# Attention and a two-layer network on one core: the network's input kept on chip as float16 parts, chunks of 256 tokens, weight scales by groups of four blocks

## The chip, the cores and the metric

The kernel runs on one core of one Trainium2 chip. A core has a matrix engine (PE), a vector engine (DVE), a scalar engine (ACT), a general engine (POOL), and a queue (SP) that issues DMAs. The metric is the time on the device in microseconds. The kernel before took 1076.19 us (median of three runs, 1075.35 to 1078.62).

## The reference

Attention over 8 batches, 8 heads, 576 positions and 64 features, with a causal mask and a decay bias from running sums of `s`; then a network of 512 to 2048 to 512 features over all 4608 tokens. All of it in float32; the two weight matrices arrive in 8-byte floats.

```python
scores = scale * np.matmul(q, k.transpose(0, 1, 3, 2))
s_pos = np.maximum(s, 0.0)
cum = np.cumsum(s_pos, axis=-1)
bias = -(cum[:, :, :, None] - cum[:, :, None, :])
scores = np.where(causal, -1000000000.0, scores + np.minimum(bias, 0.0))
attn = softmax(scores)                       # rows, with 1e-9 added to the sum
x = (attn @ v).transpose(0, 2, 1, 3).reshape(4608, 512)
h = x @ w_in
g = np.where(h > 0.0, h, np.exp(np.minimum(h, 0.0)) - 1.0)
out = g @ w_out
```

## The kernel before

All work is written down as operations (`op`), each with a priority, one or more ways (an engine and an assumed cost), and the tiles that it reads and writes. `Plan.issue` then puts them in one order: at each step it takes the operation that could start earliest by its assumed costs, and among equals the one with the lowest priority number. Every engine executes its own operations in that order, and so does SP with its DMAs. A tile has a tag and a number of buffers (`bufs`); its first writer can be issued only when a buffer of the tag, or of one of its `others`, is free.

Attention goes by pairs of heads (`j` is 0 to 3). Batches 0 to 2 are cut: their first 320 positions ("low", classes `Low`, `prepare_low`, `scoring_low`, `weighing_low`) are worked in full float32 at the start; then come batches 3 to 7 whole (`prepare`, `scoring`, `weighing`, one unit for the first 64 rows of both heads and one for each head), and last the other 256 positions of batches 0 to 2. Scores are made in PSUM banks (`score_bank`, tag `a`, two buffers; while the network isn't at work also the banks of `h` and `o0` to `o2`), the maximum is taken on DVE (L972), the exponent on ACT (L977), the weights are split into two float16 parts (L1022 to L1030), turned by DMA and multiplied with the values (L1131) into the one bank `av`. From there the result is copied to SBUF (L1143, L1145, or `psum_copy` for low units) and stored to `x_dram`, features by tokens.

The network goes by 12 chunks of 384 tokens in the order in which attention makes them. Chunk 0 is native: float32 products, each two records in the trace (L1301 for the hidden layer, L1346 for the output). It can begin as soon as a weight block is there. The other chunks take three float16 products instead of one float32 product (high by high, high by low, low by high; L1317 and L1354). For that `load_x` brings a chunk back from `x_dram`, and it is scaled by a power of two and split into `xh` and `xl` (L402 to L404 and L1270). For each of 16 blocks of 128 hidden features, `elu` and what follows take the bank of `h` through ACT and DVE: exponent (L1281), clamp (L1288 or L1292), maximum (L1326), high part (L1330 or L1332), low part (L1335). The 12 products of a block go into `h` (two banks), the 9 of its output into three banks that collect over all 16 blocks.

Weights come in 32 units of 512 KB (`load_unit`): a DMA into one of two raw tiles (tag `io`), one operation on ACT (L638) and two on DVE (L641, L644) that make float32 of 8-byte floats, and the largest magnitude (`peak`, L575 on DVE or L578 on ACT). When all 32 are there, `weight_scales` makes one scale for each matrix (two small products through PE in `scales_of`, L609 and L612), and `split_unit` makes the float16 parts (L402 or L403, then L659).

## Time and profile before

| | |
|---|---|
| median of three runs | 1076.19 us |
| profiled execution, its span | 1076.1 us |
| mean granted clock of TensorE | 0.990 |
| PE, PEld, DVE, ACT, POOL busy | 96%, 55%, 80%, 59%, 41% |
| HBM read, written | 79.66 MB, 19.32 MB |

The span is the time from the first to the last instruction of one profiled execution; nothing of note lies around it, as it equals the runs' median. Times in the profile are in microseconds, and those marked ns, or the middle number of a triple like 322/326/543, in nanoseconds. L1317 is line 1317 of the kernel. PEld is the loading of weights into the matrix engine. In a stretch's line each engine has its busy time and, in brackets, the number of its instructions; PEclk is the clock that TensorE was granted, as a share of full speed. In a group's line the name left of the arrow is the tile that is written, then the shape, the count, busy time and mean length, and behind it the idle time ahead of the group with what ended it. Ends of matmuls are modelled, so their cadence is read from their starts.

### The profile page before, as it was taken

Reading aid. Unit: us, or ns where it says so; the run is one execution under the profiler, and the core shown is the slowest. Engines: PE = TensorE matmul, PEld = TensorE weight load, DVE = VectorE, ACT = ScalarE, POOL = GpSimd, SP = SyncE. Lnnn points to the kernel's source line nnn. Section 1 sums busy time; section 2 is a strip of 40 time slices with the busy share of each in tenths; the row PEclk is TensorE's granted clock in tenths of the full one; section 3 lists DMA queues with packets and bytes.
Section 4 is the critical chain, followed back from the end, with each engine's and each line's share of the span. In section 5 each row is a group of like instructions: output and inputs, shape, how many; then the busy total and the mean of one; then the engine's idle time right before and its main releaser. Section 6 shows DMA issues by size and latency. Waiting matters only on the chain.

```text
span 1076.1 us, 19708 instructions
## 1 busy us (share of the span) xinstructions
PE 1028.8 (96%) x6014; PEld 597.0 (55%) x6014; DVE 859.3 (80%) x2216; ACT 640.2 (59%) x1511; POOL 443.2 (41%) x687
## 2 busy tenths in 40 slices
PE   8899999899799999999999999999999999999998
PEld 7555555345455555555555555555555655555554
DVE  7787988998788988898898888988898998442433
ACT  5787675547566666655656666665556566444443
POOL 6542443525365645454535545444444544000000
PEclk9999999899899999999999999999999999999999
DMA  6776889526667675675579675867765567210000
GB/s 192 216 223 203 213 213 203 139 65 142 172 149 193 149 171 136 169 179 147 120 168 191 144 162 137 195 159 167 170 168 143 143 156 148 52 60 1 30 1 30
DMA packets 295097, 156.52 MB, mean 145 GB/s; under 512 B 214200, under 2 KB 269776, under 8 KB 294992
## 3 DMA queue, kind: packets, MB, share of 16 engines
q1 hardware_dynamic: 294992, 155.27, 58.5%
q8 instruction: 48, 0.79, 0.3%
q14 instruction: 57, 0.47, 0.2%
HBM read 79.66 MB, written 19.32 MB: 92 GB/s over the span
## 4 chain that ended last, share of the span: by engine, by line
PE 70%; DVE 16%; issue 5%; DMA 4%; ACT 2%; POOL 2%; SPq 1%; DVEq 0%; POOLq 0%; ACTq 0%
PE o L1354 24%; PE h L1317 23%; PE sc L969 8%; PE av L1131 5%; DVE p L1030 4%; PE o L1346 3%; PE h L1301 2%; DVE xl L1270 2%; DVE h L1326 2%; DVE wp L659 1%; DVE gg L1335 1%; DVE p L972 1%; PE trl L791 1%; DMA T<-p 1%; DMA stq<-in_qT_dram 1%
## 5 line engine op out<-in xcount | busy, mean ns | idle before, releaser
L1317 PE MATMUL h<-xh,wp 128*128 128x384 f16 x1408 | 394.1, 329 | 19.4 <-DVE gg L1335 14.0
L1354 PE MATMUL o<-wp,gg 128*128 128x512 f16 x1584 | 390.6, 382 | 0.0
L1317 PEld LDWEIGHTS <-wp 128*128 128x128 f16 x2112 | 198.0, 98 | 177.0 <-issue 35.8
L1317 PE MATMUL h<-xl,wp 128*128 128x384 f16 x704 | 230.8, 328 | 3.9 <-DVE xl L1270 3.9
L1354 PEld LDWEIGHTS <-gg 128*128 128x128 f16 x1584 | 147.2, 99 | 154.0 <-issue 6.8
L1281 ACT ACTIVATE g<-h,cs 128x384 f32<-128x384 f32 x176 | 101.8, 578 | 156.3 <-PE h L1317 145.4
L977 ACT ACTIVATE p<-p,mn 128x192 f32<-128x192 f32 (+1 forms) x232 | 144.2, 622 | 56.6 <-DVE mn L972 49.2
L1326 DVE SCALAR_TENSOR_TENSOR h<-g,cs,h 128x384 f32<-128x384 f32 x176 | 108.5, 617 | 86.8 <-ACT g L1288 85.7
L1030 DVE SCALAR_TENSOR_TENSOR p<-p,sm,p 128x512 f16<-128x512 f32 (+3 forms) x237 | 168.9, 736 | 3.2 <-POOL p L1022 1.1
L1330 ACT ACTIVATE gg<-h 128x384 f16<-128x384 f32 x155 | 75.4, 487 | 93.2 <-DVE h L1326 91.6
L969 PE MATMUL sc<-kh,qs 128*128 128x192 f32 (+2 forms) x272 | 120.0, 444 | 7.7 <-DVE mn L972 7.3
L972 DVE CUSTOM_DVE_ANT_0 p<-sc,maskw 128x192 f32<-128x192 f32 (+1 forms) x232 | 109.6, 480 | 18.8 <-PE sc L969 14.3
L1022 POOL TENSOR_SCALAR p<-p,sm 128x512 f16<-128x512 f32 (+3 forms) x120 | 79.5, 670 | 95.5 <-DVE sm L983 34.0
L1335 DVE SCALAR_TENSOR_TENSOR gg<-h,gg 128x384 f16<-128x384 f32 x176 | 96.9, 550 | 22.0 <-ACT gg L1330 19.3
L969 PE MATMUL sc<-k,q 128*128 128x192 f32 (+2 forms) x272 | 84.4, 313 | 0.5 <-DMA q<-qs 0.5
L411 POOL TENSOR_TENSOR k<-stk,kh 64x576 fp32r<-64x576 f32 x49 | 73.1, 1492 | 24.4 <-ACT kh L392 19.9
L969 PEld LDWEIGHTS sc<-kh,qs 128*128 128x128 f32 x272 | 52.4, 192 | 35.6 <-DVE mn L972 14.5
L1288 ACT ACTIVATE g<-g 128x384 f32<-128x384 f32 x134 | 69.9, 522 | 3.7
L1026 ACT ACTIVATE p<-p,sm 128x512 f16<-128x512 f32 (+3 forms) x100 | 57.4, 594 | 18.5 <-DVE sm L983 8.2
L411 POOL TENSOR_TENSOR qs<-stq,qs 64x512 fp32r<-64x512 f32 (+1 forms) x46 | 52.4, 1139 | 34.0 <-ACT qs L392 23.5
L390 POOL TENSOR_SCALAR qs<-stq 128x256 fp32r<-128x256 f32 (+1 forms) x43 | 24.3, 566 | 88.8 <-PE sc L969 57.5
L1131 PE MATMUL av<-T,v 128*64 128x256 f16 (+5 forms) x896 | 60.2, 286 | 0.0
(179 smaller groups left out, 1414.1 us busy)
## 6 DMA issues: line engine op xcount, KB each, us to landing
stk<-in_kT_dram SPq DMA_DIRECT2D x64, 288.0 KB
va<-in_vb_dram SPq DMA_DIRECT2D x32, 320.0 KB
stq<-in_qT_dram SPq DMA_DIRECT2D x40, 256.0 KB
w_i<-in_w_in_dram SPq DMA_DIRECT2D x16, 512.0 KB
w_o<-in_w_out_dram SPq DMA_DIRECT2D x16, 512.0 KB
out_dram<-ost SPq DMA_DIRECT2D x32, 256.0 KB
x_dram<-x_None SPq DMA_DIRECT2D x20, 288.0 KB
q<-qs SPq DMA_DIRECT2D x40, 128.0 KB
```

Of the source, the lines that this page charges most:

```text
L411: ("Pool", pool_2(n), lambda: pool.tensor_tensor(dst(), src(), hi(), ALU.subtract)),
L969: pe_.matmul(view(sc.v[:, :cw]), l, r, start=n == 0, stop=n == len(pairs) - 1)
L972: op(prio, [("DVE", 84 + dve_p(cw), lambda i=i, sc=sc: dve.tensor_tensor_reduce(pt.v[:, i * cw : (i + 1) * cw], sc.v[:, :cw], mv(i * cw, c ...
L977: op(prio, [("ACT", 480 + w / 1.2, lambda: act.activation(pt.v[:, :w], pt.v[:, :w], AF.Exp, bias=mn.v[:, n - 1 : n], scale=-1.0, accum_out ...
L1022: ("Pool", 160 + 1.04 * n, lambda part=part: pool.tensor_scalar(part(t16, 0), own(part), sm.v[:, r], 1.0, ALU.mult, ALU.mult)),
L1030: ("DVE-SB", dve_2(n), lambda part=part: dve.scalar_tensor_tensor(part(t16, 1), own(part), sm.v[:, r], part(t16, 0), ALU.mult, ALU.subtract)),
L1131: pe_.matmul(av.v[w.h * HB : (w.h + 1) * HB, dst], w.values.v[:, w.h, kb, v], part(w, kb, m), start=kb == 0 and m == 0 and v == 0, stop=kb ...
L1281: op(side, [("ACT", act_c(TC) + (0 if native else 90), lambda: act.activation(g.v[:, :TC], hp.v[:, :TC], AF.Exp, scale=1.0 if native else ...
L1317: pe_.matmul(hp.v[:, :TC], weight_part(f, 0, part)[1]()[:, c * P : (c + 1) * P], xx.v[:, c, :TC], start=(c == 0 and m == 0), stop=(c == NC ...
L1326: op(side, [("DVE", dve_p(TC), lambda: dve.scalar_tensor_tensor(hp.v[:, :TC], g.v[:, :TC], by(2 if sign[0] else 1), hp.v[:, :TC], ALU.mult ...
L1335: op(side, [("DVE", dve_p(TC), lambda: dve.scalar_tensor_tensor(gg.v[:, 1, :TC], hp.v[:, :TC], 2.0**-DOWN, gg.v[:, 0, :TC], ALU.mult, ALU. ...
L1354: pe_.matmul(acc[i].v, gg.v[:, g, tb], weight_part(f, 1, part)[1](), start=(f == 0 and m == 0), stop=(f == NF - 1 and m == 2),)
```

## The change

- **x stays on chip.** `produce` writes the result of attention straight from the bank `av` (for the first 64 rows of a whole batch from SBUF) as a high and a low float16 part into tiles `xs` of 512 tokens, scaled by the power of two of its own group of values. There are two such tiles, and two more in the place of weight tiles once these are done with. `x_dram`, `load_x` and the operations on `xc` go. A run of tokens is cut where a tile ends, and at the ends of chunks that hold tokens of two scales; in such a chunk `input_scale` brings both to one scale in place. Low units load the values of a whole batch at its first pair, to have their scale, and their transposes are ordered behind that scale.
- **Chunks of 256 tokens**: 18 in place of 12, chunk 0 native as before, from a float32 tile `x_first`. Two blocks of hidden features share one bank of `h` and go through ACT and DVE together, 512 columns at a time. Hidden and output steps of one chunk run on into the next in one order. The output has two banks.
- **Weight scales by groups of four blocks.** Each group has its own scale and is split as soon as its four blocks are there; the low part may also be made on POOL. The output's high part is scaled by a factor that brings all groups to one scale (`common_scale`, which needs all four). The float32 weights lie in four tiles of two blocks each, which the second eight blocks use again, and there are four raw tiles in place of two.
- **PSUM banks**: three for scores in place of two, and none borrowed from the network.

The diff, cut to its core (of the native chunk, outputs and stores only names change with the size):

```diff
-N_ST, N_A, N_AV, N_H, N_IO, N_G, N_X, N_T, N_K, N_V = 2, 2, 1, 2, 2, 1, 1, 2, 2, 2
+N_ST, N_A, N_AV, N_H, N_O, N_IO, N_G, N_GG, N_X, N_T, N_K, N_V = 2, 3, 1, 2, 2, 2, 1, 3, 2, 2, 2, 2
+TC = 256
+NATIVE = True
+TX = 512
...
+N_RAW, N_LOW = 4, 5
+OPEN_H, OPEN_O = 0, 0
...
-W0, WD = 45, 3
-F_EARLY = 6
+W_PRIO = 45, 57, 69, 81
...
+    vs = plan.buf(sb, [P, N_LOW, n_low, D], F32, "vs", tag="va", bufs=2)
...
-    w_all = [plan.buf(sb, [P, W_GROUP, 2, 512], F32, f"wa_{g}") for g in range(NG)]
+    w_values = [plan.buf(sb, [P, 2, 2, 512], F32, f"wv_{n}", tag=f"wa_{n % 4}") for n in range(NF // 2)]
     w_parts = [plan.buf(sb, [P, W_GROUP, 2, 2, 512], F16, f"wp_{g}") for g in range(NG)]
+    w_raw = plan.buf(sb, [P, N_RAW, 512, 2], U32, "w_raw", tag=f"wp_{NG - 1}")
...
+    def weight_scales(g):
+        at = A_W + g * 2 * (W_GROUP + 1)
+        col = slice(2 * g, 2 * g + 2)
+        scales_of(-600, [(at, W_GROUP + 1), (at + W_GROUP + 1, W_GROUP + 1)], 2 * g)
         op(-600, [("DVE-SB", 100.0, lambda: power(
-            scales.v.bitcast(U32)[:, 3:4], scales.v.bitcast(U32)[:, 1:2], 2 * 127))],
-           [(scales, 0)], [(scales, 3)])
+            wc.v.bitcast(U32)[:, col], scales.v.bitcast(U32)[:, col], 2 * 127))],
+           [(scales, 2 * g)], [(wc, ("inverse", g))])
+    def common_scale():
+        def steps():
+            a, b = (scales.v[:, m : 2 * NG : 2] for m in range(2))
+            ab, least, back, first, r = (wc.v[:, m : n] for m, n in ((8, 12), (12, 13), (13, 14), (14, 15), (16, 20)))
+            dve.tensor_tensor(ab, a, b, ALU.mult)
+            dve.tensor_reduce(least, ab, mybir.AxisListType.X, ALU.min)
+            power(wc.v.bitcast(U32)[:, 13:14], wc.v.bitcast(U32)[:, 12:13], 2 * 127)
+            dve.tensor_scalar(first, scales.v[:, 0:1], back, 2.0**DOWN, ALU.mult, ALU.mult)
+            power(wc.v.bitcast(U32)[:, 16:20], wc.v.bitcast(U32)[:, 8:12], 2 * 127)
+            dve.tensor_scalar(r, r, least, 2.0**-DOWN, ALU.mult, ALU.mult)
+        op(-600, [("DVE-SB", 500.0, steps)], [(scales, 2 * g) for g in range(NG)], [(wc, "common")])
...
+        def in_place():
+            pool.tensor_scalar(value(), value(), scales.v[:, col], 1.0, ALU.mult, ALU.mult)
+            pool.tensor_tensor(low_v(), value(), high_v(), ALU.subtract)
+        op(prio, [
+            ("DVE-SB", dve_2(512), lambda: dve.scalar_tensor_tensor(
+                low_v(), value(), scales.v[:, col], high_v(), ALU.mult, ALU.subtract)),
+            ("Pool", pool_1(512) + pool_2(512), in_place),
+        ], [(scales, at), high], [place, low])
...
+            if f % W_GROUP == W_GROUP - 1:
+                weight_scales(f // W_GROUP)
+                for m in range(f - W_GROUP + 1, f + 1):
+                    split_unit(m, 0)
+                    split_unit(m, 1)
+        common_scale()
...
+    xs = [plan.buf(sb, [P, 2, NCB, TX], F16, f"x_{k}", tag="x", bufs=N_X,
+                   others=[(f"wa_{m}", 1, lambda n: n > 1) for m in range(2)], always=True)
+          for k in range(-(-at // TX))]
+    x_parts = [[] for _ in xs]
...
+    x_first = plan.buf(sb, [P, NCB, TC], F32, "x_first")
...
+    def spans(t0, n):
+        cuts = {t0, t0 + n}
+        for t in range(t0 // TC * TC, t0 + n, TC):
+            if t > t0 and (t % TX == 0 or len(domains(t // TC)) > 1 or len(domains(t // TC - 1)) > 1):
+                cuts.add(t)
+        cuts = sorted(cuts)
+        return list(zip(cuts, cuts[1:]))
+    def produce(prio, j, t0, n, src, reads, by, on_psum=True):
+        fixed = isinstance(by, float)
+        scale = (lambda: by) if fixed else by
+        for lo, up in spans(t0, n):
+            k, m, o = lo // TX, up - lo, lo % TX
+            x, key = xs[k], (j, lo)
+            if NATIVE and lo < TC:
+                psum_copy(prio, m, lambda lo=lo, up=up: x_first.v[:, j, lo:up],
+                          lambda lo=lo, up=up: src()[:, lo - t0 : up - t0], reads[:1], [(x_first, (j, lo))])
+                continue
+            x_parts[k].append((lo, up, j, key))
+            def dst(part, x=x, o=o, m=m):
+                return x.v[:, part, j, o : o + m]
+            def of(lo=lo, up=up):
+                return src()[:, lo - t0 : up - t0]
+            more = 0 if fixed else 90
+            if on_psum:
+                op(prio, [
+                    ("ACT", act_c(m) + more, lambda dst=dst, of=of: act.activation(
+                        dst(0), of(), AF.Copy, scale=scale())),
+                    ("DVE", dve_p(m), lambda dst=dst, of=of: dve.tensor_scalar(
+                        dst(0), of(), scale(), None, ALU.mult)),
+                ], reads, [(x, (0, *key))])
+            else:
+                scaled(prio, m, lambda dst=dst: dst(0), of, scale, reads, [(x, (0, *key))])
+            op(prio, [("DVE" if on_psum else "DVE-SB", dve_p(m), lambda dst=dst, of=of: dve.scalar_tensor_tensor(
+                dst(1), of(), scale(), dst(0), ALU.mult, ALU.subtract))],
+               reads + [(x, (0, *key))], [(x, (1, *key))])
...
+        if j == 0:
+            first = A_LOW + b * (NP + 1)
+            for n in range(NP):
+                r = (b * NP + n) % N_LOW
+                load(prio, lambda r=r: vs.v[:, r], lambda n=n: vb[b, n, :, :n_low], [], [(vs, r)], P * n_low * D * 4)
+                peak(prio, n_low * D, lambda r=r: vs.v[:, r], [(vs, r)], first + n, mybir.AxisListType.XY)
+            low_scale[b] = group_scale(prio, first, S_LOW + 2 * b)
...
+            produce(prio, u.j, start[u.b, False], LOW, lambda: av.v[:, :LOW], [av, (scales, col)],
+                    lambda: scales.v[:, col : col + 1])
...
+        va = plan.buf(sb, [P, NP, 2 * (NQ + 1), D], F32, f"va_{at}", tag="va", bufs=2)
...
-                        others=[("h", N_H, opening(NF)), ("o0", 1, opening(1)), ("o1", 1, opening(1)),
-                                ("o2", 1, opening(2))])
+                        others=[("h", N_H, opening(OPEN_H)), ("o", N_O, opening(OPEN_O))])
...
+            produce(prio, u.j, u.start + HB * (first == 0), wq, lambda: av.v[:, :wq], [av], 2.0**-15)
...
+        for m, (lo, up, _) in enumerate(parts):
+            x, o = xs[lo // TX], lo % TX
+            keys = [(part, *key) for a, e, _, key in x_parts[lo // TX] if a < up and e > lo for part in range(2)]
+            op(side, [("DVE-SB", 100 + 0.55 * 8 * (up - lo), lambda x=x, o=o, n=up - lo, m=m: dve.tensor_scalar(
+                x.v[:, :, :, o : o + n], x.v[:, :, :, o : o + n], cs.v[:, 1 + m : 2 + m], None, ALU.mult))],
+               [(cs, "input")], [(x, key) for key in keys])
...
+        steps = [(0, fp) for fp in range(NF // 2) if NATIVE]
+        steps += [(ch, 2 * g + q) for ch, g in EARLY for q in range(2)]
+        steps += [(ch, fp) for ch in range(NATIVE + N_EARLY, N_CH) for fp in range(NF // 2)]
...
+            hp = plan.buf(ps, [P, 2, TC], F32, f"h_{ch}_{fp}", tag="h", bufs=N_H)
+            for m in range(2):
+                f = 2 * fp + m
+                for c in range(NCB):
+                    def step(m=m, f=f, c=c):
+                        ops = ((0, 0), (0, 1), (1, 0))
+                        for i, (part, xx) in enumerate(ops):
+                            pe_.matmul(
+                                hp.v[:, m], weight_part(f, 0, part)[1]()[:, c * P : (c + 1) * P],
+                                x.v[:, xx, c, o : o + TC],
+                                start=(c == 0 and i == 0), stop=(c == NCB - 1 and i == 2),
+                            )
+                    op(main(ch), [("PE", 3 * pe16(TC), step)],
+                       [(x, (part, *key)) for *_, j, key in parts if j == c for part in range(2)]
+                       + [weight_part(f, 0, part)[0] for part in range(2)], [hp])
+            def by(m):
+                return cs[ch].v[:, m + g : m + g + 1]
+            def down():
...
+                return 2.0**-DOWN if early else wc.v[:, 16 + g : 17 + g]
+            more = [] if early else [(wc, "common")]
+            gt = plan.buf(sb, [P, 2 * TC], F32, f"g_{ch}_{fp}", tag="g", bufs=N_G)
+            op(side, [("ACT", act_c(2 * TC) + 90, lambda: act.activation(
+                gt.v, flat(hp.v), AF.Exp, scale=by(BACK)))], [hp, (cs[ch], g)], [gt])
...
+            gg = plan.buf(sb, [P, 2, 2, TC], F16, f"gg_{ch}_{fp}", tag="gg", bufs=N_GG)
+            op(side, [("DVE", dve_p(2 * TC), lambda: dve.scalar_tensor_tensor(
+                flat(hp.v), gt.v, by(MINUS if sign[0] else FIRST), flat(hp.v), ALU.mult, ALU.max))],
+               [gt, (cs[ch], g)], [hp])
             op(side, [
+                ("ACT", act_c(2 * TC) + (0 if early else 90), lambda: act.activation(
+                    flat(gg.v[:, 0]), flat(hp.v), AF.Copy, scale=down())),
+                ("DVE", dve_p(2 * TC), lambda: dve.tensor_scalar(
+                    flat(gg.v[:, 0]), flat(hp.v), down(), None, ALU.mult)),
+            ], [hp] + more, [(gg, 0)])
+            op(side, [("DVE", dve_p(2 * TC), lambda: dve.scalar_tensor_tensor(
+                flat(gg.v[:, 1]), flat(hp.v), down(), flat(gg.v[:, 0]), ALU.mult, ALU.subtract))],
+               [hp, (gg, 0)] + more, [(gg, 1)])
...
+                acc = [plan.buf(ps, [P, DM], F32, f"o_{ch}_{fp}_{i}", tag="o", bufs=N_O) for i in range(2)]
...
+        order = [("hidden", 0)]
+        for n in range(1, len(steps)):
+            order += [("hidden", n), ("project", n - 1)]
+        order.append(("project", len(steps) - 1))
+        order.remove(("hidden", len(steps) - 1))
+        order.insert(order.index(("project", len(steps) - 3)), ("hidden", len(steps) - 1))
...
-    for w in w_all:
-        plan.place(w)
     attention()
-    rows = []
-    for b, blocks in pieces:
-        start = HB + P * blocks[0] if blocks[0] else 0
-        rows.append((b, blocks[0] > 0, start, HB + P * len(blocks) + P * blocks[0] - start))
-    chunks = []
-    while rows:
-        chunk, left = [], TMAX
-        while left:
-            b, late, r, n = rows.pop(0)
-            if n > left:
-                rows.insert(0, (b, late, r + left, n - left))
-                n = left
-            chunk.append((b, late, r, n))
-            left -= n
-        chunks.append(chunk)
-    load_weights(0, F_EARLY)
-    xc = load_x(0, chunks[0])
-    load_weights(F_EARLY, NF)
-    weight_scales()
-    for f in range(NF):
-        split_unit(f, 0)
-        split_unit(f, 1)
-    for ch, rows in enumerate(chunks):
-        xc = moe_chunk(ch, rows, xc, lambda: load_x(ch + 1, chunks[ch + 1]) if ch + 1 < len(chunks) else None)
+    load_weights(0, NF)
+    network()
...
```

More of the change, by code (lines that the diff above doesn't have):

```diff
@@ new lines, with domains @@
+    for b, blocks in pieces:
+        late = blocks[0] > 0
+        start[b, late] = at
+        n = P * len(blocks) + HB * (not late)
+        low = not late and b < N_CUT
+        domain.append((at, at + n, S_LOW + 2 * b if low else S_GROUP + 2 * groups.index((b, late))))
+        at += n
+    N_CH = at // TC
+    N_EARLY = len({ch for ch, _ in EARLY})
+    def domains(ch):
+        lo, up = ch * TC, ch * TC + TC
+        return [(max(a, lo), min(e, up), col) for a, e, col in domain if a < up and e > lo]
@@ L1363, in moe_chunk @@
-        steps = []
-        for f in range(NF):
-            if f == NF - 1 and end:
-                steps = project(f - 2)
-                steps.pop(0)()
-            (hidden_native if native else hidden)(f)
-            for step in steps:
-                step()
-            steps = []
-            if f > 0 and not (end and f == NF - 2):
-                for step in project(f - 1):
-                    step()
-        for step in project(NF - 1):
-            step()
-        following = after()
@@ new lines, in network, with store @@
+        held = {}
+        def store(ch, i, src, reads):
+            for lo, up, _ in domains(ch):
+                b, late = next(k for k, t in start.items() if t <= lo < t + S and any(
+                    a == t and e >= up for a, e, _ in domain))
+                lo, up = max(lo, ch * TC + i * P), min(up, ch * TC + i * P + P)
+                if lo < up:
+                    r0 = b * S + late * LOW + lo - start[b, late]
+                    o = slice(lo - ch * TC - i * P, up - ch * TC - i * P)
+                    load(-1000 + ch, lambda r0=r0, n=up - lo: out[r0 : r0 + n, :], lambda o=o: src()[o],
+                         reads, [], (up - lo) * DM * 4)
```

468 lines of the change are left out of this document (235 added, 233 removed).

## The prediction

> **What bounds the kernel now.** The profiled execution took 1076.1 us and the three runs have a median of 1076.19, so the sum is made against 1076.1 as it stands. About 0.3% (3 us) is what a measurement of this kernel can tell from no change. I read the page's engine shares first, then busy time by stretches, then the first and last use of the tiles that mark the stages, then the chain of waits.
>
> ```profile
> PE 1028.8 (96%) x6014; PEld 597.0 (55%) x6014; DVE 859.3 (80%) x2216; ACT 640.2 (59%) x1511; POOL 443.2 (41%) x687
> ```
>
> ```profile
> core 0: us, PE busy (x) PEld busy (x) DVE busy (x) ACT busy (x) POOL busy (x), PEclk, DMA share, GB/s
> 0.00:25.00 25.00, 21.86 (x146) 18.91 (x147) 20.53 (x62) 12.33 (x37) 15.46 (x47) 1.00 0.64 190
> 25.00:50.00 25.00, 21.13 (x135) 13.43 (x134) 18.08 (x70) 18.07 (x61) 13.79 (x33) 1.00 0.68 197
> 50.00:75.00 25.00, 23.91 (x148) 15.25 (x148) 22.63 (x80) 21.61 (x70) 12.83 (x29) 1.00 0.77 230
> 75.00:100.00 25.00, 23.50 (x117) 12.65 (x113) 19.55 (x62) 19.13 (x56) 7.13 (x18) 1.00 0.71 218
> 100.00:150.00 50.00, 49.54 (x193) 27.98 (x193) 42.25 (x108) 33.11 (x83) 18.52 (x26) 1.00 0.79 210
> 200.00:250.00 50.00, 44.72 (x240) 23.77 (x240) 47.04 (x94) 23.07 (x55) 11.50 (x16) 0.97 0.36 99
> 250.00:300.00 50.00, 43.17 (x252) 25.01 (x248) 41.68 (x116) 30.86 (x72) 24.23 (x37) 0.90 0.70 168
> 950.00:1000.00 50.00, 50.00 (x271) 26.27 (x269) 16.25 (x32) 20.55 (x39) 0.00 (x0) 1.00 0.11 32
> ```
>
> PE is the bound nearly everywhere, and near the end it has no hole at all. Holes lie in the first 100 us and from 200 to 300, where DVE is at 94% and the granted clock falls to 0.90. The stages:
>
> ```profile
> L378 SPq DMA_DIRECT2D w_o<-in_w_out_dram x16: 327/359/577, 15.3 to 170.0; - x16
> L644 DVE SCALAR_TENSOR_TENSOR wa<-w_o x16: 673/689/951, 33.1 to 176.7; 128x512 uint32<-128x512 uint32 x16
> L659 DVE SCALAR_TENSOR_TENSOR wp<-wa,scales,wp x32: 735/741/1885, 184.5 to 231.2; 128x512 f16<-128x512 f32 x32
> L378 SPq DMA_DIRECT2D x_dram<-xl x12: 327/378/539, 24.6 to 103.7; - x12
> L378 SPq DMA_DIRECT2D x_dram<-x x12: 333/352/523, 747.9 to 933.3; - x12
> L1317 PE MATMUL h<-xh,wp x1408: 322/326/543, 190.1 to 1066.3; 128*128 128x384 f16 x176
> L1354 PE MATMUL o<-wp,gg x1584: 376/379/650, 198.0 to 1071.5; 128*128 128x512 f16 x198
> ```
>
> So the low attention runs until 104 us, weights arrive until 177, their split is a burst on DVE from 184 to 231, the first half-precision product comes at 190.1, attention is over at 933, and 138 us of network alone follow.
>
> **The price of the streams.** In the stretch without holes I read the cadence of the matmuls, since their ends are modelled:
>
> ```profile
> 1000.43 0.49 PE L1317 MATMUL h<-xh,wp 128*128 128x384 f16 x2
> 1000.92 0.49 PE L1317 MATMUL h<-xh,wp 128*128 128x384 f16 x2
> 1001.41 1.77 PEld L1354 LDWEIGHTS <-gg 128*128 128x128 f16 x9
> 1001.57 2.10 PE L1354 MATMUL o<-wp,gg 128*128 128x512 f16 x9
> ```
>
> Two xh and one xl fill the 0.49 us from one line to the next: 163 ns for 384 columns. Nine of 512 columns take 2.10 us, of which 0.38 is the last one's own length: 215 ns. The line through both is 0.41 ns a column plus some 5 ns at most; I take 162.5, 215.8 and, between them and the origin, 109 ns for 256 columns. The native products:
>
> ```profile
> 103.88 2.58 PE h L1301 x8
> 106.46 2.57 PE o L1346 x6
> ```
>
> One weight block costs 5.15 us for 384 tokens, so 16 of them 82.4; for 256 tokens two thirds, 55.0. Before, half precision has 2112 h at 162.5 (343.2) and 1584 o at 215.8 (341.8): 685.0. After, 17 chunks have 192 h and 96 o each: 3264 at 109 (355.8) and 1632 at 215.8 (352.2): 708.0. Network on PE before: 767.4; after: 763.0. Six more scale chains with two small products each give back some 3 us. **The work of PE changes by about -1 us.** The change can only pay by closing holes.
>
> One thing could spoil the 109: weight loads take 98 ns each, and there are 1152 more. But loads overlap one another too:
>
> ```profile
> 53.60 0.38 PE L791 MATMUL trl<-ident,pl 128*128 128x128 f32 x2
> 53.82 0.38 PE L791 MATMUL trl<-ident,p 128*128 128x128 f32 x2
> L791 PEld LDWEIGHTS trl<-ident,pl 128*128 128x128 f32 x60 | 7.9, 141 | 3.8 <-POOL pl L990 2.1 <-ACT pl L994 1.3 <-DVE pl L992 0.5
> ```
>
> These transposes go every 110 ns (two in 0.22) though each load is recorded with 141 ns. So a load's record is longer than what it costs the stream, and 109 holds.
>
> **The first stage decides.** Before: 190.1 us until half precision starts, 685.0 of it, 4.4 after the last matmul's start (1076.1 less 1071.7), and 196.6 left over for attention and holes in between. The native chunk shrinks by 27.4 us in the first stage, and 23.0 of half precision come back in the second. If half precision still started at 190, this would be a loss. So the question is what sets 190. It is the weights: from 100 us on PE is full only because native work is there as each block lands. And what paces the weights?
>
> ```profile
> 73.81 0.38 SPq L378 DMA_DIRECT2D w_i<-in_w_in_dram  x1
> 80.24 0.38 SPq L378 DMA_DIRECT2D w_i<-in_w_in_dram  x1
> 87.41 0.38 SPq L378 DMA_DIRECT2D w_i<-in_w_in_dram  x1
> 96.05 0.38 SPq L378 DMA_DIRECT2D w_i<-in_w_in_dram  x1
> 73.81 4.45 DMA w_i<-in_w_in_dram
> L641 DVE TENSOR_SCALAR w_i<-w_i x16: 398/428/651, 19.7 to 167.3; 128x512 uint32<-128x512 uint32 x16
> L575 DVE TENSOR_REDUCE peaks<-wa 128x1 f32<-128x512 f32 x16 | 10.8, 677 | 0.2
> L1301 PE MATMUL h<-x,wa x128: 483/486/590, 63.4 to 183.3; 128*128 128x384 f32 x128
> ```
>
> Each of the two raw tiles (one for w_in, one for w_out by turns) is issued anew after 6.4 to 8.6 us: a landing of 4.45 us (the chain has it), then conversion and peak. That is latency with two tiles, not bandwidth: the DMA share is 0.68 to 0.79 there. The change gives four raw tiles (N_RAW), so up to twice the pace, and it stops where something else is full. DMA: 32 units of 512 KB in the 162 us from 15 to 177 are 104 GB/s of some 205; filling the last quarter of the share lets weights go at some 165 GB/s, 102 us for all, until about 120. DVE: busy 81 us in the first 100, of which 16 units took some 24 for weights (0.43 and 0.69 each, and 9 of their peaks), so 57 are its own. Add all conversions (32 at 0.43 and 0.69: 36), 16 peaks (11), the splits that now fall into this stage (32 at 0.74: 24), the native chunk's elementwise work (8 steps, about 8) and the x parts (about 5): 141 us, which at DVE's 94% of the burst is 150. PE: 90 busy in the first 100 (native, from 63.4 on, has a part of that), say 80 for the low attention, 55 native and 7 for a pair of heads make some 140. **I take 150 for the start of half precision; bounds 120 and 190.** The split needs no burst any more, since each group has its own scale; its Pool way lowers the 150 rather than raising it. Eight blocks have tiles at first, and the other eight wait until a native step and a split have freed one; I assume that they keep up (see the second rival).
>
> **Later.** Attention that PE did before 190 and now does after 150: of the 100 to 150 stretch it is what native work (18 a 25 us) leaves, some 4 a quarter, so +7. Holes ahead of the network:
>
> ```profile
> L1317 PE MATMUL h<-xh,wp 128*128 128x384 f16 x1408 | 394.1, 329 | 19.4 <-DVE gg L1335 14.0 <-ACT xh L403 3.4 <-DVE wp L659 1.4
> L1317 PE MATMUL h<-xl,wp 128*128 128x384 f16 x704 | 230.8, 328 | 3.9 <-DVE xl L1270 3.9
> L1270 DVE SCALAR_TENSOR_TENSOR xl<-xc,cs,xh 128x384 f16<-128x384 f32 x44 | 36.0, 847 | 2.8 <-POOL xh L402 2.7
> L1335 DVE SCALAR_TENSOR_TENSOR gg<-h,gg 128x384 f16<-128x384 f32 x176 | 96.9, 550 | 22.0 <-ACT gg L1330 19.3
> ```
>
> The xh, xl and wp holes (8.7) go with the chunk-wise split. Of the 14.0 behind gg a part goes, because a step now has 24*109+12*216 = 5.2 us for an elementwise chain that grows by five times some 0.1, where it had 3.9. I take -12, bounds -23 and +5 (what a bank of two blocks, held longer, may cost). The lower granted clock, 0.97 and 0.90 over 50 us each, is about 6 us of PE time; where no burst empties PE it should not fall. [...]
>
> The rest lies beside PE. No x goes to DRAM and back (44 stores, 76 loads); that was hidden, for the one long piece in the chain is this, about a hole counted above:
>
> ```profile
> 274.75 4.67 DMA x_dram<-x_None
> ```
>
> The x parts are now two reads of the bank where there were one read and two operations from SBUF: DVE loses xl (36.0) and copies, gains 94 low parts (33), about half of the high parts (19) and eight microseconds of rescaling in six mixed chunks; steps of 512 save it a little (136 gg at some 0.68 for 176 at 0.550: 4). About even; POOL loses 18. What hides a slip here is attention's lead, the 138 us of network after 933; without that cover 15 us would show as 15. At most four x tiles of 512 tokens hold attention back to some 2000 tokens ahead; the lead at 933 is about 138/62.3*384 = 850.
>
> Sum: 150 + 708.0 + (196.6 + 7 - 12) + 4.4 = 1054.0. **Forecast 1054 us**, with 1040 to 1070 as the likeliest case's own range (start 140 to 160, holes -18 to -5).
>
> **Rivals.** *Weights come no sooner.* If DMA or conversion, not the two tiles, sets the pace, half precision starts at 187; PE idles where native work stood, and attention, which DVE at 85% paces, moves up by some 6: 187 + 708.0 + (196.6 - 6 - 12) + 4.4 = 1078. For it: DMA at 0.79 is not far from full. Against it: the reissue of a raw tile right behind its conversion.
>
> *The four weight tiles close a loop (slower).* Blocks 8 to 15 load only into tiles that native steps 0 to 3 and their splits have left. A native step is 6.9 us of PE, and until 104 us low attention fills PE (21 to 24 busy of 25). If a step comes every 25 us from 60 on, step 3 ends at 160; four units land and convert (13 us), a scale chain and split follow (7), and step 7 (6.9): start 187 at the earliest, and with a stall at each turn 200: 200 + 708.0 + (196.6 - 4 - 10) + 4.4 = 1095. It is slower than before once step 3 is projected after about 148. For it: the order puts the network behind everything else. Against it: native work began at 63.4 amid the low attention, and x for the first 256 tokens needs batch 0 alone, the first four of the twelve stores from 24.6 to 103.7, at 7.2 each by about 46, where 384 needed batch 1.
>
> *Short products don't hide their loads.* Were the 98 ns of a load in the open, the 1152 more products would cost 113 us, 1167 in all; if a fifth of it showed, 1077. Against it are the transposes at 110 ns with loads of 141, and nine loads inside nine products whose 215 ns are their 512 columns alone. [...]
>
> *More is won*: a start at 130 and all 23 of holes gone: 130 + 708.0 + (196.6 + 10 - 23) + 4.4 = 1026. For it: POOL's way of the split and ACT's peaks can take work from DVE. Against it: DVE's 141 us do not fit into 130 without that.
>
> **Numbers.** Forecast 0.58; no sooner 0.15; loop 0.14; loads exposed 0.03; more won 0.10. Faster (under 1073): 0.57 of the first, 0.10 of the last, 0.01 elsewhere: 0.68. Same (1073 to 1079): 0.01, 0.09 and 0.02, 0.12. Slower: 0.06 and 0.14, 0.20. The range 1037 to 1083 leaves out most of more won and of the loop.
>
> **What would show it.** The last wa before 150 (right) or near 177 (first rival); raw tiles reissued every 6 to 8 us four at a time; the last native o below 150; first wp parts before 100; h of 256 columns every 109 ns; no DVE stretch at 94% with PE below 45 of 50; holes ahead of h under 12 us. Wrong would be a first half-precision product at 185 or later, a load of block 8 later than 100, or new waits of PE on the score banks, which are three throughout where idle network banks helped before.

## The result, and the profile after

| | before | after | one priority (below) |
|---|---|---|---|
| median | 1075.77 us (1073.75 to 1078.62) | 1090.6 us (1085.46 to 1090.94) | 1056.81 us (1055.99 to 1057.59) |
| ratio to before | | 1.0126, 95% interval 1.01 to 1.0152 | 0.9834, 0.9804 to 0.9863 |
| profiled span | 1076.1 us | 1088.5 us | 1054.2 us |

The change made the kernel slower by 1.3%, where 1054 us, a faster kernel, were forecast. The third column runs ahead: the changed kernel with one line edited, which is where most of the answer came from.

The page of after, engine shares; then its stretches before and behind the first half-precision product, with the columns as in the prediction:

```profile
PE 1037.9 (95%) x7284; PEld 713.3 (66%) x7284; DVE 875.9 (80%) x2276; ACT 619.9 (57%) x1411; POOL 423.5 (39%) x657
```

```profile
0.00:169.00 169.00, 151.17 (x823) 103.79 (x824) 145.32 (x454) 110.82 (x301) 60.37 (x134) 0.96 0.52 158
169.00:1088.50 919.50, 886.73 (x6463) 609.49 (x6461) 730.63 (x1823) 509.07 (x1110) 363.16 (x523) 0.99 0.55 121
```

The same two stretches of before:

```profile
0.00:190.10 190.10, 180.04 (x882) 110.10 (x883) 158.99 (x479) 130.11 (x363) 86.80 (x182) 1.00 0.76 207
190.10:1076.10 886.00, 848.78 (x5134) 486.89 (x5132) 700.32 (x1738) 510.12 (x1149) 356.38 (x506) 0.99 0.55 132
```

Half precision does start sooner, at 169.0 in place of 190.1. But PE idles 17.8 us ahead of that (169.00 less 151.17) where it idled 10.1, and 32.8 behind it where it idled 37.2, and it runs at a lower clock in both: granted were 0.96 for 1.00 ahead of it, and 0.986 for 0.988 behind it. A ledger of the whole span makes this plain. I split each span into PE's idle time, the time lost to a halved clock (a granted share of 0.50 in the trace; half the length of each such stretch, without one that begins behind the last matmul), the dummy transposes that fill idle PE early on (`fillers`, L1593 in after, L1417 in before), and what is left: the work itself.

| us | start of half precision | idle before, behind it | half clock before, behind it | dummies | work of PE | span |
|---|---|---|---|---|---|---|
| before | 190.1 | 10.1, 37.2 | 0, 10.2 | 14.1 | 1004.5 | 1076.1 |
| after | 169.0 | 17.8, 32.8 | 6.8, 11.9 | 19.5 | 999.7 | 1088.5 |
| one priority | 162.8 | 18.8, 12.3 | 3.4, 0 | 19.6 | 1000.1 | 1054.2 |

The change takes 4.8 us of work from PE. The first stage wastes 19.9 us more than before (idle 7.7, half clock 6.8, dummies 5.4; the dummies all lie in the first 60 us), and the long second stage only 2.7 less. With the 4.8 us of work that makes the 12.4 us between the spans.

Where the second stage's idle time comes from is in the groups, and in the waits of PE there (total, times, longest):

```profile
L1449 PE MATMUL h<-x,wp 128*128 128x256 f16 x3264 | 400.6, 274 | 22.4 <-DVE gg L1488 22.2
L1512 PE MATMUL o<-wp,gg 128*128 128x512 f16 x1632 | 393.0, 386 | 1.9 <-ACT gg L1483 1.6 <-DVE sm_None L1094 0.2
```

```profile
PE h L1449 <- DVE gg L1488: 22.2, 13, 4.5
PE sc L1081 <- DVE mn L1084: 3.0, 6, 0.7
PE o L1512 <- ACT gg L1483: 1.6, 1, 1.6
```

Holes behind xh, xl and wp have gone, as forecast. The 14.0 us behind gg didn't shrink, they became 22.2. They aren't spread evenly: of the eleven holes over 0.4 us ahead of a hidden product, nine, with 19.8 us, end 9.0 to 16.1 us behind the first hidden product of a chunk, each of another chunk; the eight other chunks in half precision have no hole over 0.4 us there, and why they are spared isn't shown. Here is one, the last chunk's, where no attention is left to disturb the picture; first PE, then DVE and ACT of the same microseconds:

```profile
1035.79 0.49 PE L1449 MATMUL h<-x,wp 128*128 128x256 f16 x3
1036.12 2.75 PE L1512 MATMUL o<-wp,gg 128*128 128x512 f16 x12
1038.71 1.80 PE L1449 MATMUL h<-x,wp 128*128 128x256 f16 x15
1040.35 2.75 PE L1512 MATMUL o<-wp,gg 128*128 128x512 f16 x12
1042.94 3.77 PE L1449 MATMUL h<-x,wp 128*128 128x256 f16 x33
1047.75 0.50 PE L1449 MATMUL h<-x,wp 128*128 128x256 f16 x3 [1.05 <-DVE gg L1488]
1048.09 2.75 PE L1512 MATMUL o<-wp,gg 128*128 128x512 f16 x12
```

```profile
1044.84 0.43 DVE L1475 TENSOR_SCALAR g<-g 128x512 f32<-128x512 f32 x1 [4.95 <-ACT g L1466]
1045.37 0.76 DVE L1479 SCALAR_TENSOR_TENSOR h<-g,cs,h 128x512 f32<-128x512 f32 x1
1046.94 0.75 DVE L1488 SCALAR_TENSOR_TENSOR gg<-h,wc,gg 128x512 f16<-128x512 f32 x1 [0.81 <-ACT gg L1483]
```

```profile
1044.12 0.69 ACT L1466 ACTIVATE g<-h,cs 128x512 f32<-128x512 f32 x1 [0.29 <-PE h L1449]
1046.22 0.69 ACT L1483 ACTIVATE gg<-h,wc 128x512 f16<-128x512 f32 x1 [1.41 <-DVE h L1479]
```

A hidden step is 24 products. At 1038.71 the new chunk's first step gets 15 of them, then come the 12 products of the old chunk's last output step, then 33: the missing 9 and the whole second step. The elementwise chain of the first step runs from 1044.12 to 1047.69, 3.6 us. Inside a chunk an output step and a hidden step (2.6 us each) lie between a step's last hidden product and its own output, and 3.6 fits. Here only the second hidden step does. Both banks of `h` are then full, and PE waits 1.05 us. While attention uses DVE and ACT too, the same place costs 1.1 to 4.5.

The order has a reason in the code. The list of steps puts the next chunk's first hidden step ahead of the old chunk's last output step. But `main = lambda ch: 10000 + ch` (L1370, the expression of L1248 before) gives the older chunk the lower number, so its output step, once ready, is put in between the hidden products that are still to come.

### The profile page after: what moved, and what is told of

It is laid out like the page before. It is cut to its first block, busy times and chain, and to the rows that moved or that the text cites. A ratio compares the mean times of both kernels' runs of the same rounds, so it can differ in the third digit from the quotient of the medians.

```text
span 1088.5 us, 21856 instructions
## 1 busy us (share of the span) xinstructions
PE 1037.9 (95%) x7284; PEld 713.3 (66%) x7284; DVE 875.9 (80%) x2276; ACT 619.9 (57%) x1411; POOL 423.5 (39%) x657
## 4 chain that ended last, share of the span: by engine, by line
PE 70%; DVE 19%; issue 4%; ACT 3%; DMA 2%; POOL 1%; SPq 0%; DVEq 0%; POOLq 0%; ACTq 0%
PE o L1512 27%; PE h L1449 25%; PE sc L1081 8%; PE av L1247 5%; DVE p L1142 3%; DVE h L1479 2%; DVE p L1084 2%; PE h L1387 1%; PE o L1416 1%; DVE gg L1488 1%; DVE wp L695 1%; DVE peaks L581 1%; DVE wv L673 1%; PE trl L906 1%; PE avl L922 1%
## 5 line engine op out<-in xcount | busy, mean ns | idle before, releaser
L1449 PE MATMUL h<-x,wp 128*128 128x256 f16 x3264 | 400.6, 274 | 22.4 <-DVE gg L1488 22.2
L1449 PEld LDWEIGHTS <-wp 128*128 128x128 f16 x3264 | 306.8, 98 | 92.8 <-DVE gg L1488 27.3
L1089 ACT ACTIVATE p<-p,mn 128x192 f32<-128x192 f32 (+1 forms) x232 | 143.9, 621 | 68.1 <-DVE mn L1084 66.6
L1466 ACT ACTIVATE g<-h,cs 128x512 f32<-128x512 f32 x136 | 93.1, 685 | 123.8 <-PE h L1449 123.0
L1483 ACT ACTIVATE gg<-h,wc 128x512 f16<-128x512 f32 x121 | 82.9, 685 | 100.7 <-DVE h L1479 99.5
L1488 DVE SCALAR_TENSOR_TENSOR gg<-h,wc,gg 128x512 f16<-128x512 f32 x136 | 101.3, 745 | 25.1 <-ACT gg L1483 24.1
L1479 DVE SCALAR_TENSOR_TENSOR h<-g,cs,h 128x512 f32<-128x512 f32 x136 | 102.1, 751 | 9.8 <-ACT g L1471 3.8
L1081 PE MATMUL sc<-kh,qs 128*128 128x192 f32 (+2 forms) x272 | 106.2, 398 | 3.2 <-DVE mn L1084 3.0
L1475 DVE TENSOR_SCALAR g<-g 128x512 f32<-128x512 f32 x70 | 34.9, 499 | 66.5 <-ACT g L1466 66.0
L391 POOL TENSOR_SCALAR qs<-stq 128x512 fp32r<-128x512 f32 (+1 forms) x41 | 26.7, 651 | 92.3 <-PE sc L1081 38.5
L1247 PEld LDWEIGHTS <-v 128*64 128x64 f16 x896 | 44.8, 110 | 21.0 <-issue 8.2
```

The source lines that it names most:

```text
L1081: pe_.matmul(view(sc.v[:, :cw]), l, r, start=n == 0, stop=n == len(pairs) - 1)
L1089: op(prio, [("ACT", 480 + w / 1.2, lambda: act.activation(pt.v[:, :w], pt.v[:, :w], AF.Exp, bias=mn.v[:, n - 1 : n], scale=-1.0, accum_out ...
L1247: pe_.matmul(av.v[w.h * HB : (w.h + 1) * HB, dst], w.values.v[:, w.h, kb, v], part(w, kb, m), start=kb == 0 and m == 0 and v == 0, stop=kb ...
L1449: pe_.matmul(hp.v[:, m], weight_part(f, 0, part)[1]()[:, c * P : (c + 1) * P], x.v[:, xx, c, o : o + TC], start=(c == 0 and i == 0), stop= ...
L1466: op(side, [("ACT", act_c(2 * TC) + 90, lambda: act.activation(gt.v, flat(hp.v), AF.Exp, scale=by(BACK)))], [hp, (cs[ch], g)], [gt])
L1479: op(side, [("DVE", dve_p(2 * TC), lambda: dve.scalar_tensor_tensor(flat(hp.v), gt.v, by(MINUS if sign[0] else FIRST), flat(hp.v), ALU.mul ...
```

## The experiments

All times are medians beside runs of the kernel before on the same chip (1074.9 to 1075.7).

### The order across a chunk's end

**One priority for the products of all chunks.**

```diff
-        main = lambda ch: 10000 + ch
+        main = lambda ch: 10000
```

> The changed kernel, with one priority for all of the network's products instead of one that grows with the chunk. Theory A, that the holes of 22.4 us ahead of h stand at the ends of chunks, because an output step of the older chunk is put into the middle of the next chunk's first hidden step: the holes ahead of h fall under 5 us, the half-clock stretches behind them go, and the time falls by 18 to 28 us, to 1062 to 1072. Rival, that these holes come from ACT and DVE being busy with attention when a chunk ends: the holes stay at 15 us or more and the time within 5 us of 1090.

Measured: 1056.81 us, ratio 0.9834 (0.9804 to 0.9863), 33.8 us below the changed kernel as it was, more than the 18 to 28 of theory A. Groups, and PE at a chunk's end:

```profile
L1449 PE MATMUL h<-x,wp 128*128 128x256 f16 x3264 | 397.2, 273 | 0.9 <-DVE gg L1488 0.9
```

```profile
162.80:1054.20 891.40, 879.06 (x6476) 608.86 (x6475) 729.44 (x1853) 502.45 (x1095) 370.70 (x533) 1.00 0.57 125
```

```profile
958.74 2.78 PE L1449 MATMUL h<-x,wp 128*128 128x256 f16 x24
961.36 2.75 PE L1512 MATMUL o<-wp,gg 128*128 128x512 f16 x12
963.95 2.78 PE L1449 MATMUL h<-x,wp 128*128 128x256 f16 x24
966.57 2.75 PE L1512 MATMUL o<-wp,gg 128*128 128x512 f16 x12
```

A chunk begins at 963.9 here, and nothing shows it: 24 and 12 go on by turns. The holes ahead of h fall from 22.4 to 0.9 us, and no half clock is left behind the start. By the ledger 20.5 us of idle time and 11.9 of half clock in the second stage are gone, 32.4 of the 34.3 us between the spans.

**A third bank for the hidden sums, with the old priorities.** It leaves the order as it is and takes away what makes the order hurt. The price is a score bank.

```diff
-N_ST, N_A, N_AV, N_H, ... = 2, 3, 1, 2, ...
+N_ST, N_A, N_AV, N_H, ... = 2, 2, 1, 3, ...
```

> The changed kernel with its own priorities, but three banks of PSUM for the hidden sums instead of two, and two for the scores instead of three. Theory A (PE waits at a chunk's end because both banks of hidden sums are full while the elementwise chain of the first hidden step began 2.6 us late): a third bank holds one more hidden step, 2.6 us of products, so that most single waits of 1.2 to 2.8 us go: holes ahead of h under 8 us instead of 22.4. The two score banks cost the attention something that the same theory can't price; bounds 0 and 30 us, so 1062 to 1100, and the holes tell, not the time. Rival (the waits come from VectorE being behind with other work, and a bank more only moves them): holes ahead of h stay at 15 or more.

Measured: 1072.13 us, ratio 0.9957 (0.9939 to 0.9975), 18.5 below the changed kernel as it was.

```profile
L1449 PE MATMUL h<-x,wp 128*128 128x256 f16 x3264 | 402.6, 273 | 2.2 <-DVE x L1344 1.9 <-DVE gg L1488 0.2
```

```profile
1017.62 1.80 PE L1449 MATMUL h<-x,wp 128*128 128x256 f16 x15
1019.26 2.75 PE L1512 MATMUL o<-wp,gg 128*128 128x512 f16 x12
1021.85 5.40 PE L1449 MATMUL h<-x,wp 128*128 128x256 f16 x48
1027.09 2.75 PE L1512 MATMUL o<-wp,gg 128*128 128x512 f16 x12
```

The old chunk's 12 output products still stand behind 15 hidden ones, but then 48 hidden ones run without a hole. Of 22.2 us behind gg 0.2 are left. So the holes need both the order and two banks, and VectorE isn't behind with its work; the rival falls.

**Both together.**

> Both cures together: one priority for all chunks' products, and three banks for the hidden sums with two for the scores. Theory A (both close the same holes, and the one priority has closed nearly all of them, 0.9 us left): the third bank has nothing more to give, and the lost score bank costs what it cost beside the kernel's own order, so 1060 to 1078, slower than with the one priority alone at 1056.8. Rival (the third bank's gain is one of its own, a later start of the hidden chain that is forgiven anywhere): 1040 to 1052.

Measured: 1074.41 us (0.9992, 0.9966 to 1.0017). The time is theory A's. The second stage idles 16.7 us and loses 6.8 to half clock, more than with one priority alone, and the first idles 21.6 with 10.2 of half clock. The cures don't add. PE waits longer for a score bank to be read:

```profile
PE sc L1081 <- DVE mn L1084: 8.2, 16, 1.2
```

With one priority alone that is 4.0 us over the whole span, which fits the missing bank. That the rest of the 17.6 us between the two medians comes from it too isn't shown.

**One priority in the kernel before.**

```diff
-        side, main = -1000 + ch, 10000 + ch
+        side, main = -1000 + ch, 10000
```

> The kernel before, with one and the same priority for the network's products of all chunks in place of a later one for each chunk; nothing else differs. Theory A (the order of the products across a chunk's end is one weakness that both kernels share, and it costs the old kernel less, because its first hidden step of a chunk keeps PE busy for twice as long): the old kernel's holes ahead of h that wait for gg are 14.0 us in all, and some of these lie inside the stage of single precision or in the attention, so the gain is 3 to 12 us: 1063 to 1072, and the holes ahead of h<-xh,wp fall from 19.4 to 8 to 14. Rival (the order alone is worth what the run of the changed kernel with one priority gained, whatever the kernel): 30 us or more, 1045 or less, and then the change itself would be worth nothing. Second rival (the old kernel needs the priorities by chunk, since its chunks wait for parts of x): slower than before by 3 or more.

Measured: 1074.7 us, ratio 0.9993 (0.997 to 1.0015). None of the theories had this: in the two traces every engine has the same instructions in the same order (of PE's 6014 matmuls only four, of one `av` group, are recorded in another order, and the loads that belong to them are not). In the old list a chunk's last output step stands ahead of the next chunk's first hidden step anyway, so the number by chunk decided nothing. It began to decide when the change let the steps run on across chunks. The weakness wasn't shared; it came with the change, from a line that the change took over. What makes the old kernel's own 14.0 us behind gg stays open.

### The first stage

**Score banks borrowed as before** (`OPEN_H, OPEN_O = 8, 2` in place of `0, 0`), **two raw tiles** (`N_RAW = 2` in place of 4), and **the low parts of the split on GpSimd**, each on the changed kernel alone:

```diff
+        tmp = plan.buf(sb, [P, 512], F32, f"sp_{f}_{kind}", tag="sp")
+        def aside():
+            pool.tensor_scalar(tmp.v, value(), scales.v[:, col], 1.0, ALU.mult, ALU.mult)
+            pool.tensor_tensor(low_v(), tmp.v, high_v(), ALU.subtract)
         op(prio, [
-            ("DVE-SB", ...), ("Pool", ..., in_place),
+            ("Pool", pool_1(512) + pool_2(512), aside),
```

> The changed kernel, but scores may borrow the two banks of h until the native chunk has taken its eight, and the two of the output until the native chunk takes them, as before. Theory B, that three banks slow the low attention: the last x part of a low unit comes at 150 or earlier instead of 169, half precision starts at 150 to 155, and the time falls by 12 to 18 us. Rival, that DVE (95% busy from 50 to 150) sets the first stage: the start of half precision stays within 5 us of 169, and the time within 5 us of 1090.

> The changed kernel with two raw weight tiles instead of four. If the two tiles paced the weights before the change, the last converted weight comes near 175 instead of 134, half precision starts at 185 or later instead of 169, and the time rises by 8 to 20 us. If DMA or DVE paces them, the last weight stays below 145 and the time within 4 us of 1090.

> The changed kernel with the low float16 parts of the weights made on POOL alone, from a tile of its own; DVE is rid of 32 operations of some 0.74 us, 24 us in all, before half precision starts. If DVE sets the first stage: half precision starts 12 to 24 us earlier than 169 and the time falls by 10 to 22 us. If the banks or the loads set it: the start within 5 us of 169, the time within 5 us of 1090. POOL, at some 2 us for each part, would take 64 us for them over 100 us, and could become what the last group waits for: then the start comes later than 169.

Measured: 1113.7 us (1.0361, 1.0311 to 1.0411), 1113.23 (1.0356, 1.0314 to 1.0398) and 1096.67 (1.0202, 1.0163 to 1.0241). The start of half precision came at 204.4, 203.2 and 138.5. The low parts of the split (first and last start), of the second run and then of the changed kernel as it was:

```profile
L695 DVE SCALAR_TENSOR_TENSOR wp<-wv,scales,wp x32: 736/745/1273, 60.2 to 188.9; 128x512 f16<-128x512 f32 x32
```

```profile
L695 DVE SCALAR_TENSOR_TENSOR wp<-wv,scales,wp x32: 733/744/1273, 50.4 to 148.9; 128x512 f16<-128x512 f32 x32
```

With two raw tiles the last conversion starts at 173.1, against 133.7 with four, and the last split at 188.9, against 148.9: the raw tiles do pace the weights, at a price of 22.6 us, more than the 8 to 20 expected. With borrowed banks neither theory B nor its rival held: the low attention ends at 124.5 in place of 166, but the first native output product comes at 123.1 instead of 58.5, the last conversion at 172.5, and half precision 35 us later. So in this stage one thing is bought with another. And the third run starts 30 us sooner, more than expected, and ends 6 us later, which no theory had: its second stage idles 43.2 us and loses 18.8 to the clock. An early start is not itself a gain, since PE's work hardly changes with the order (999.7 and 1000.1 us in the ledger, after and with one priority).

**The same questions with the order mended**: low parts on GpSimd for all tiles (the edit above), or for the second product's tiles alone (the same where `kind == 1`); the split behind the loads of its own group instead of ahead of everything, on VectorE; and no low parts made. The last two in short:

```diff
-        prio, at = -500 + f, 2 * (f // W_GROUP)
+        prio, at = W_PRIO[f // W_GROUP] + 20 + f % W_GROUP, 2 * (f // W_GROUP)
```

```diff
-            ("DVE-SB", ... low_v(), value(), scales.v[:, col], high_v(), ALU.mult, ALU.subtract)),
+            ("Pool-M", pool_1(512), lambda: pool.memset(low_v(), 0.0)),
```

> The changed kernel with one priority for all chunks' products, and with the low parts of the weights' split on GpSimd (multiply into a tile of its own, then subtract), not on VectorE. Theory A (the low parts on VectorE are what holds the first product of half precision at 163 to 169; but the first chunk then runs ahead of its weights, as the run with GpSimd alone did, which began at 138.5 and reached the same point later): first product at 136 to 145, holes in the first chunk of half precision 10 to 25 us, and a time of 1050 to 1064, the same as with the one priority alone. Rival (GpSimd's run lost only by the order at the chunks' ends, which is mended here): the 24 us of the earlier start are kept, 1030 to 1040. Second rival (GpSimd's lateness costs the attention of the middle too): 1065 or more.

> One priority for all chunks' products, and the low parts of half of the weights' tiles (those of the second product) on GpSimd into a tile of their own, the others on VectorE. Theory A (first stage is a trade between VectorE, the low attention and the weights): first product at 148 to 160 and 1050 to 1064, not to be told from the one priority alone. Rival (the moved 12 us of VectorE come out at the end): 1042 to 1049.

> The changed kernel with one priority for all chunks' products, and with the weights' split no longer ahead of all else on VectorE (priority -500) but behind the loads and conversions of its own group and the low attention's steps of that time; both parts on VectorE. Theory A (the four bursts of the split on VectorE, at 49 to 56, 82 to 88, 110 to 120 and 139 to 149, are what pushes the low attention from 104 to 166): the low attention ends at 120 to 150; the first product of half precision comes no sooner than 160 and up to 185, since the same work is done in all; the time is 1050 to 1066. Rival (VectorE's order in the first stage is a loss by itself, not a trade): first product at 150 or sooner with the low attention ended by then too, 1040 to 1046.

> The changed kernel with one priority for all chunks' products, and without the subtraction that makes the low parts of the weights: GpSimd fills them with zeros early, so that the 23.6 us of the 32 subtractions on VectorE are left out (the products are all still made, with zeros in the place of the low parts). Theory A (VectorE's work up to the first product of half precision sets that product): it comes at 138 to 150 instead of 163, and the time falls by as much as the start, to 1035 to 1047. Rival (the start is set by the loads of the weights or by PE's own work of single precision, and VectorE's share is hidden behind them): first product at 158 or later, 1052 to 1060. Second rival (the start comes sooner, but the work that was waiting is only done later, as with the low parts on GpSimd): first product at 138 to 150 and 1050 or more.

| us | start | idle before, behind it | half clock before, behind it | median | ratio to before |
|---|---|---|---|---|---|
| one priority | 162.8 | 18.8, 12.3 | 3.4, 0 | 1056.81 | 0.9834 |
| and low parts on GpSimd | 141.1 | 14.1, 27.1 | 3.4, 6.8 | 1071.56 | 0.9954 (0.9935 to 0.9973) |
| and half of them there | 173.0 | 24.9, 17.6 | 10.2, 0 | 1069.53 | 0.9951 (0.9932 to 0.997) |
| and the split later | 170.1 | 22.3, 15.5 | 5.1, 0 | 1065.37 | 0.9894 (0.9863 to 0.9926) |
| and no low parts made | 154.3 | 14.7, 16.8 | 5.1, 0 | 1053.72 | 0.9803 (0.9775 to 0.983) |

The run with all low parts on GpSimd has theory A's start, 141.1, but not its time (1050 to 1064), and the run with half of them there has neither. With all of them there the second rival holds, by its time: the idle time turns up behind it, 7.1 us behind gg and 5.2 behind one transfer of attention's weights. With half of them there the start comes later, not sooner. The later split has theory A's start and time, but the low attention ended at 164, not by 150. The last run's start lies between theory A's and the first rival's, and its time is one that both rivals had: without 23.6 us of subtractions the start comes 8.5 us sooner, and the median is 3.1 us lower, with intervals that overlap. Its VectorE is as busy over the whole span as with the one priority alone (872.1 us and 2300 operations): 32 subtractions less, and 27 other operations that could have gone to ACT or GpSimd.

```profile
PE 1021.0 (97%) x7267; PEld 707.5 (67%) x7267; DVE 872.2 (83%) x2295; ACT 614.4 (58%) x1382; POOL 414.7 (39%) x667
```

None of these beats the one priority clear of noise, even with work left out. One caution holds for all of them: each edit reorders the whole program, and what such a reordering is worth by itself wasn't measured. So differences of some 10 us between these five runs settle nothing about the theories.

## Why the prediction was wrong

By the terms of the forecast's sum the 1088.5 us are 169.0 + 708.0 + 207.1 + 4.4. The start is 19.0 us later than forecast, and the rest, for which 191.6 stood, 15.5 longer; the cadence of the products was right. (The last matmul of before starts at 1071.5, not at 1071.7; that cancels in the sum.)

**The step that failed** is the term "-12" for holes, with bounds of -23 and +5. It argued that a step of 5.2 us covers a longer elementwise chain. That is so inside a chunk, as the one-priority run shows. At a chunk's end the order has another pattern, and there 2.6 us have to cover 3.6. I had read that the steps "run on into the next in one order", but not what the number by chunk does to that order. Behind gg alone the holes grew by 8.2 us (22.2 for 14.0), against 8.7 us of the xh, xl and wp holes that did go: ahead of the hidden products 23.3 us became 22.4. So the term came out at -0.9, which is 11.1 of the 15.5. That lies within its bounds; what failed is the reason for the -12.

**The clock** was the second failure: "where no burst empties PE it should not fall". Half clock rose from 10.2 to 18.7 us in all, 6.8 of it ahead of the start, and of the nine stretches in after seven come right behind 3.41 us in which PE was busy for only 22 to 43% (the last section has the count).

**The start, 150, was mis-sized**, though the size of VectorE's work was right. By 150 us VectorE had been busy for 136.0 us, 91% of the time, and its last low part of the weights was made at 149.6. Half precision came 19 us later, and in these PE was full and VectorE half idle:

```profile
75.00:100.00 25.00, 22.73 (x109) 15.93 (x108) 22.83 (x65) 18.55 (x51) 8.73 (x17) 0.86 0.55 172
100.00:150.00 50.00, 43.25 (x202) 28.19 (x200) 47.77 (x156) 32.37 (x83) 18.81 (x34) 0.97 0.31 100
150.00:169.00 19.00, 17.88 (x85) 10.21 (x86) 9.27 (x32) 10.83 (x29) 4.64 (x8) 0.91 0.21 57
```

Those are PE, its loads, VectorE, ACT and GpSimd in turn. The forecast took 150 us of VectorE and 140 of PE as running side by side, and the longer one as the start. But from 75 to 150 VectorE is full (70.6 us of 75) and PE isn't, where before it was the other way (42.25 and 49.54 of 50 from 100 to 150), and PE's low attention waits behind it. The low attention ended at 166 us instead of 104, and PE's largest wait in the first 169 us is for its probabilities (`pl`):

```profile
L922 PE MATMUL avl<-tl,vs x144: 218/326/432, 20.8 to 166.1; 128*64 128x256 f32 x48, 128*64 128x192 f32 x48, 128*64 128x64 f32 x48
```

```profile
PE trl L885 <- POOL pl L1102: 7.4, 3, 4.3
```

The longest of these three waits ends at 151.1, and ahead of it stand eight low parts in a row on VectorE, then the sum (`sml`) that the probabilities are divided by:

```profile
144.25 5.38 DVE L695 SCALAR_TENSOR_TENSOR wp<-wv,scales,wp 128x512 f16<-128x512 f32 x8
150.70 0.37 POOL L1102 TENSOR_SCALAR pl<-pl,sml 128x128 f32<-128x128 f32 x1 [8.94 <-DVE sml L1095]
151.12 0.33 PE L885 MATMUL trl<-ident,pl 128*128 128x128 f32 x1 [4.26 <-POOL pl L1102]
```

Moving the split later didn't mend this (start 170.1), so what order of this stage would is open.

"Its Pool way lowers the 150" was wrong: all 32 low parts went to VectorE (the row of L695 with four raw tiles).

**The form of the sum** hid this. I wrote that PE's work changes by -1 us and that the change can only pay by closing holes, and that was near (-4.8). Then I added up a start, a stream and a remainder, as if an earlier start were worth its length. It isn't: 138.5 and 162.8 gave 1096.67 and 1056.81.

**What was right.** Hidden products of 256 columns come every 109 ns, 24 in 2.62 us, and 12 output products in 2.59: the rival of loads in the open falls, since each of these hidden products has a load recorded with 98 ns (the mean of 3264) and still follows the one before it by 109. Four raw tiles bring the weights sooner: the last conversion starts at 133.7, against 176.7, and the first float16 parts are made at 49; "weights come no sooner" falls. The loop over the four weight tiles gave 1095, near the number measured, by a mechanism that wasn't there: block 8 was loaded from 66.6 on, not behind 100. Score banks weren't waited for more than before (3.0 us in the second stage, for 7.1). So none of the three signs that were to show the forecast wrong came. Three of those that were to show it right stayed out: the last native output product starts at 168.5, not below 150; VectorE was busy for 47.77 of the 50 us from 100 to 150, with PE at 43.25; and the holes ahead of h were 22.4 us, not under 12.

That one edited line brings 1056.81, 2.8 us from the forecast, doesn't make the forecast right. Its start is 12.8 us later than forecast and the rest 12.6 shorter (179.0 for 191.6): that they cancel is luck.

## What to carry to other kernels

Where PE's work doesn't change, make the sum over its idle time, stage by stage, and count an earlier start as nothing until the work behind it is shown to move up. When a list of steps is made to run across a boundary, look for every priority, tag or buffer that still counts by the old unit, and write out the order of two steps on either side of it. A chain that fits between two steps needs to be checked at the one place where only one step lies between.

## What the runs showed of the hardware

Behind some holes PE ran at half clock (a granted share of 0.50), so that they cost more than their length. The stretches of half clock are all multiples of 3.41 us, but for those that the trace's end cuts: 3.41 and 10.24 us in before, 3.41 and 6.83 in after. Their starts lie whole multiples of 3.41 us apart in each of these two. I cut the spans of all thirteen kernels, this case's two and the eleven experiments, into windows of that length in step with these stretches, and took PE's busy share of each. Of the windows at full clock (from 25 us on), all 50 with PE busy for less than 45% were followed by one at half clock (4 of them in before and 7 in after, with PE busy for 9 to 43%). Of some 40 with 45 to 58% about a quarter were (one of 6 in before and after), and of some 3800 above that fewer than ten (one of 582 in these two); these two counts shift a little with how exactly the windows are laid. One of the 50, in after, around the hole of 2.70 us at 566:

```profile
565.00:568.50 3.50, 1.20 (x11) 0.82 (x9) 3.43 (x9) 2.55 (x5) 1.39 (x1) 1.00 0.58 138
568.50:572.00 3.50, 3.11 (x9) 1.35 (x10) 2.18 (x6) 0.69 (x1) 0.37 (x1) 0.51 0.91 198
```

And one of 2.34 us at 625 that falls across two windows, with no half clock behind it:

```profile
623.10:626.50 3.40, 1.80 (x17) 1.37 (x14) 3.24 (x13) 2.26 (x5) 1.00 (x3) 1.00 0.86 212
626.50:629.90 3.40, 2.66 (x14) 1.39 (x15) 2.09 (x4) 1.11 (x2) 0.00 (x0) 1.00 1.04 196
```

So the hole of 2.70 us, most of it in one window, cost another 1.7 us (half of 3.41), and that of 2.34 us, across two, cost none. What makes the clock go by such windows isn't shown.
